# Second-phase weights of a three-stage network: raw slots, decoding order, store times and tile addresses

## Chip, cores and metric

The kernel runs on one core of a Trainium2 chip. The metric is the device time of one execution in microseconds (us); smaller is better.

## Reference

Three layers follow each other on 3072 tokens (4 batches of 768) with 384 features, all in float32:

```python
def _attn_ref(q, k, v, alpha):            # 8 heads of 48
    for t in range(S):
        state = alpha[:, :, t, :, None] * state + np.einsum('bhd,bhe->bhde', k[:, :, t], v[:, :, t])
        y[:, :, t] = np.einsum('bhd,bhde->bhe', q[:, :, t], state)
def _moe_ref(x, w_in, w_out):             # d_ff 2048
    h = x @ w_in
    return (h * (1.0 / (1.0 + np.exp(-h)))) @ w_out
def _moe2_ref(x, w_gate, w_val, w_out):   # d_ff 1536
    g = x @ w_gate
    return (g * (1.0 / (1.0 + np.exp(-g))) * (x @ w_val)) @ w_out
```

The result is `_moe2_ref(_moe_ref(_attn_ref(...)))`.

## The kernel before, in words

Every float32 product is made of three matmuls: both operands are split into a high part (rounded to the matmul's own float32 form) and the low rest, and high by high, low by high and high by low are added in PSUM. In names, `gh`, `ah` and `w` hold high parts and `gl` and `al` low ones.

**First phase.** Attention runs in chunks of 128 tokens. Beside it, and after it, runs the first feed-forward layer, in seven blocks of 4, 3, 3, 3, 3, 4 and 4 chunks, so its matmuls are 512 or 384 columns wide. One step of a block takes 128 of the 2048 hidden features: `g1` makes nine matmuls into `h` (L642, L643, L645), `act1` takes the silu on ACT twice (once rounded into `gh`, once in place) and leaves `gl` = `h` − `gh` to DVE (L264), and `g2` makes nine more (L676, L677 with `gh`, the last three at L679 with `gl`). After each half of a step, `slot` does whatever else is due. The first layer's weights `w` stay in SBUF.

**Second phase.** The gated layer is computed in three passes over 1024 tokens. A pass has 12 groups (`group`), each of 33 matmuls of 128x512 at L820, by a scheme of the Strassen kind: the stationary operands are sums and differences of weight blocks (tile `comb`, 128 x 2304, high and low half), the moving ones are sums and differences of tokens (`mov`). In a group, ACT copies (L854, L856, L867) and DVE adds (`u4` at L860, `v` at L873) stand between the matmuls, and `use` (L835, L838) makes the products `a` of the gate's silu and the values. Then the pass's output part follows: 24 steps of nine matmuls (`og`, L901), 216 in all, with the output weights `wo`; before each, `osplit` rounds one `a` tile to `ah` on ACT and takes `al` on DVE, or, in the first pass and for half of the steps, on POOL.

**The weights of the second phase.** They lie packed in DRAM, a float32 in 8 bytes, as 36 units of 128 x 768 words (24 of gate and value, 12 of output weights). A unit is loaded by SP (L610, 384 KB), then decoded by DVE in three integer steps over 128x384, all in SBUF (step 0 L47 `dec<-raw`, step 1 L52 `raw<-raw,dec`, step 2 L57 into `f` or back into `raw`). Two units make one `f` tile; POOL adds its blocks up (`combine`, L791 to L794), ACT rounds nine blocks into the high half of `comb` (`high_comb`, L798, 128x1152), POOL takes the low half (`low_comb`, L264, 128x1152), and SP stores `comb` to DRAM (L803, 1152 KB). The first pass uses `comb` as it is made; the other two load it back (`fetch_comb`, L807). An output unit is decoded, rounded by ACT (`high_wo`, L811) and subtracted by POOL (`low_wo`, 128x384).

**What orders this.** The order is written out by hand: each engine runs its instructions in the order in which the program issues them. `units2` (L1011) is one tick of the weights' work: each step of the chain advances by at most one unit in a tick, later steps first, and a step takes only what an earlier tick left. In a tick, a unit is loaded only if at most one loaded unit is still undecoded (`st["d2"] + 1`) and a slot of the three is free (`free + 2`). Ticks come from `slot` in the last two blocks of the first phase, from the first pass's groups through `spare` (one after `u4`, one at the group's end) and `need2`, and from its output part, in every second step (`b == 0`) or as often as the next `wo` needs. The load of the tokens of the next pass (`load_x1`, L708, tile `x1r` in the buffer `big1`) and the POOL and ACT work on them (`moving_steps`, L728) lie among them. `comb` tiles go in turn to two buffers of pool `sp2` and, every third, to `big0`.

## Time and profile before

| what | us |
|---|---|
| median of 3 executions | 1048.15 (1042.44 to 1048.27) |
| profiled execution, its own time | 1045.21 |
| its span | 1043.4 |
| PE busy in it | 977.0 |
| DVE, ACT, POOL busy | 516.9, 432.5, 273.3 |
| mean granted TensorE clock | 0.978 of full speed |

The profiled execution lies 2.9 us below the median of the three, and its span 1.8 us below its own time. PE is TensorE's matmuls, PEld its weight loads, and SPq is the DMA queue of SyncE. A matmul's own time in the trace overlaps the next one's start, so the pace of matmuls is read from start to start. A granted clock of 1.00 is 2.4 GHz, and a stretch at less is a mixture with 1.2 GHz.

### The profile page before, as it was taken

To read this page: it belongs to the slowest core of one execution; us is meant where nothing else is said; L and a number is where in the kernel's file an instruction comes from. 1 tells how busy PE (TensorE), PEld (TensorE's weight loads), DVE (VectorE), ACT (ScalarE), POOL (GpSimd) and SP (SyncE) were. 2 spreads that over 40 slices of the span, in tenths; PEclk is the share of its full clock that TensorE was granted. 3 is DMA by queue.
4 is the path that set the end of the run, shared out by engine and by line. 5 is a ranking of instruction groups with operands and counts; after the bars stand their busy time and mean duration, and the time that the engine had idled before them with its cause. 6 is when DMAs were issued, how large, how long until landed. Compare 5 with 4: busy or idle time off the path is not lost.

```text
span 1043.4 us, 14192 instructions
## 1 busy us (share of the span) xinstructions
PE 977.0 (94%) x5317; PEld 814.9 (78%) x5317; DVE 516.9 (50%) x912; ACT 432.5 (41%) x977; POOL 273.3 (26%) x347
## 2 busy tenths in 40 slices
PE   9889999999999999999599987988799999999995
PEld 5667798799999998888377765866588878788784
DVE  8889936444343553434342575664133354333432
ACT  3544435545454554433223543534233434433322
POOL 5434416343231441401330353254100020000000
PEclk9899999999999999999899998999899999999998
DMA  7664003222212222004620366441146420435001
GB/s 245 238 241 132 6 3 123 79 85 54 65 50 75 82 82 69 21 1 121 227 91 30 136 214 224 152 182 46 60 143 235 142 87 1 151 137 180 2 1 63
DMA packets 32780, 111.54 MB, mean 107 GB/s; under 512 B 3648, under 2 KB 7232, under 8 KB 28096
## 3 DMA queue, kind: packets, MB, share of 16 engines
q1 hardware_dynamic: 32224, 110.11, 31.2%
q8 instruction: 43, 0.70, 0.3%
q10 hardware_dynamic: 480, 0.46, 0.2%
q14 instruction: 33, 0.27, 0.1%
HBM read 85.00 MB, written 23.59 MB: 104 GB/s over the span
## 4 chain that ended last, share of the span: by engine, by line
PE 71%; DMA 10%; DVE 9%; issue 5%; POOL 3%; ACT 2%; SPq 0%; DVEq 0%; POOLq 0%; ACTq 0%
PE o L901 14%; PE u L820 13%; DMA raw<-in_w_dram 8%; PE p L820 7%; PE h L642 5%; PE x L679 5%; PE h L643 5%; PE h L645 5%; PE x L676 5%; PE x L677 5%; PE y L483 2%; PE y L505 2%; DVE f L57 2%; POOL w L264 2%; DVE dec L47 1%
## 5 line engine op out<-in xcount | busy, mean ns | idle before, releaser
L820 PE MATMUL u<-mov,comb 128*128 128x512 f32 x756 | 189.1, 397 | 12.7 <-DVE u L860 9.7
L820 PEld LDWEIGHTS u<-mov,comb 128*128 128x128 f32 x756 | 142.8, 191 | 48.2 <-DVE u L860 12.3
L901 PE MATMUL o<-ah,wo 128*128 128x512 f32 x432 | 140.2, 405 | 8.0 <-POOL wo L264 7.0
L642 PE MATMUL h<-x,w 128*128 128x384 f32 (+1 forms) x336 | 125.0, 372 | 1.7 <-DMA x<-y 1.6
L659 ACT ACTIVATE gh<-h 128x384 fp32r<-128x384 f32 (+1 forms) x112 | 59.7, 533 | 157.7 <-PE h L645 157.3
L676 PE MATMUL x<-gh,w 128*128 128x384 f32 (+1 forms) x336 | 122.9, 366 | 1.7 <-ACT gh L659 1.6
L643 PE MATMUL h<-x,w 128*128 128x384 f32 (+1 forms) x336 | 123.4, 367 | 0.0
L264 DVE TENSOR_TENSOR gl<-h,gh 128x384 fp32r<-128x384 f32 (+1 forms) x112 | 68.5, 612 | 108.5 <-ACT h L660 105.5
L677 PE MATMUL x<-gh,w 128*128 128x384 f32 (+1 forms) x336 | 122.0, 363 | 0.0
L820 PE MATMUL p<-mov,comb 128*128 128x512 f32 x432 | 110.8, 391 | 2.4 <-DVE a L838 2.3
L901 PEld LDWEIGHTS o<-ah,wo 128*128 128x128 f32 x432 | 83.2, 193 | 29.6 <-POOL wo L264 8.2
L679 PE MATMUL x<-gl,w 128*128 128x384 f32 (+1 forms) x336 | 88.2, 371 | 17.8 <-DVE gl L264 17.8
L820 PEld LDWEIGHTS p<-mov,comb 128*128 128x128 f32 x432 | 81.2, 188 | 21.0 <-DVE a L838 3.7
L901 PE MATMUL o<-al,wo 128*128 128x512 f32 x216 | 87.3, 404 | 4.3 <-DVE al L264 4.3
L891 ACT ACTIVATE ah<-a 128x512 fp32r<-128x512 f32 x72 | 45.5, 632 | 101.9 <-PE o L901 95.4
L645 PE MATMUL h<-x,w 128*128 128x384 f32 (+1 forms) x336 | 86.3, 365 | 0.0
L679 PEld LDWEIGHTS x<-gl,w 128*128 128x128 f32 x336 | 61.0, 189 | 29.3 <-DVE gl L264 23.1
L264 DVE TENSOR_TENSOR al<-a,ah 128x512 fp32r<-128x512 f32 x60 | 44.7, 745 | 72.0 <-ACT ah L891 69.6
L352 POOL TENSOR_TENSOR kq<-in,r 128x256 f32<-128x256 f32 x47 | 35.4, 754 | 157.6 <-DVE r L341 152.2
L47 DVE TENSOR_SCALAR dec<-raw 128x384 int32<-128x384 int32 x64 | 41.5, 648 | 63.7 <-DMA raw<-in_w_dram 62.5
L642 PEld LDWEIGHTS h<-x,w 128*128 128x128 f32 x336 | 64.0, 190 | 11.3 <-issue 5.4
L676 PEld LDWEIGHTS x<-gh,w 128*128 128x128 f32 x336 | 63.4, 189 | 10.1 <-ACT gh L659 4.2
(130 smaller groups left out, 1529.8 us busy)
## 6 DMA issues: line engine op xcount, KB each, us to landing
comb<-comb_d SPq DMA_DIRECT2D x24, 1152.0 KB, 5.2
raw<-in_w_dram SPq DMA_DIRECT2D x64, 384.0 KB, 3.9
in<-in_pk_dram SPq DMA_DIRECT2D x22, 770.5 KB, 4.2
comb_d<-comb SPq DMA_DIRECT2D x12, 1152.0 KB, 6.1
in_v<-in_pk_dram SPq DMA_DIRECT2D x24, 256.0 KB, 3.2
x1r<-x_d SPq DMA_DIRECT2D x6, 768.0 KB, 7.5
out_dram<-ob SPq DMA_DIRECT2D x18, 256.0 KB, 2.2
x_d<-x1e SPq DMA_DIRECT2D x4, 576.0 KB, 3.3
```

What stands on the lines that cost most here:

```text
L47: eng.tensor_scalar(out=tmp, in0=high, scalar1=3, scalar2=0x3FFFFFF8, op0=ALU.logical_shift_left, op1=ALU.bitwise_and,)
L264: eng.tensor_tensor(out=lo, in0=src, in1=hi.bitcast(F32), op=ALU.subtract)
L642: PE.matmul(acc, part(u, k), xh, start=(k == 0), stop=False)
L643: PE.matmul(acc, part(u, k, 1), xh, start=False, stop=False)
L645: PE.matmul(acc, part(u, k), xl, start=False, stop=(k == len(xk) - 1))
L659: ACT.activation(out=gh, in_=hb, func=AF.Silu)
L676: PE.matmul(x1_t[j][m], part(u, m), gh, start=(f == 0), stop=False)
L677: PE.matmul(x1_t[j][m], part(u, m, 1), gh, start=False, stop=False)
L679: PE.matmul(x1_t[j][m], part(u, m), gl, start=False, stop=(f == NF1 - 1))
L820: PE.matmul(acc, s[:, hs, i], x[:, hx], start=start and n == 0, stop=n == 2, skip_group_check=True,)
L891: ACT.activation(out=ah, in_=a, func=AF.Copy)
L901: PE.matmul(o_t[b][m], part(wo_t[f], m, l), x, start=(f == 0 and n == 0), stop=(f == NF2 - 1 and n == 2),)
```

## The change

The packed weights get one tile `raw2` with four slots, in the buffer `big1`, which `x1r` leaves for `big0`; all `comb` tiles now come from pool `sp2`. In a tick up to two loads are issued, as far as slots are free (`free + 3` with the next one). A unit is decoded if it was loaded at least two ticks earlier, and then all three integer steps are issued in a row (`decode2`). The store of `comb` becomes a step of its own (`keep_comb`), one tick after `low_comb`. In the first pass, a group of even number makes both its ticks after `u4`, and one of odd number makes one there and none at its end; ticks that are lacking come from `need2` ahead of the next group. In the first pass's output part every step has a tick. The small tiles `lim`, `cnt`, `ones` and `tot` share a tile of tag `y3`.

```diff
@@ -237,6 +237,8 @@
     x1_d = dram.tile([128, KT, NT], F32, name="x1_d")
     comb_d = dram.tile([NF2, 128, 18 * 128], F32, name="comb_d")
     cp = ctx.enter_context(tc.tile_pool(name="cp", bufs=1))
+    edge = ctx.enter_context(tc.tile_pool(name="edge", bufs=1, side="right"))
+    edge.tile([128, 120], F32, name="edge_r")
     wstack = ExitStack()
     wp = wstack.enter_context(tc.tile_pool(name="wp", bufs=2 * NF1, side="right"))
     ps = ctx.enter_context(tc.tile_pool(name="ps", bufs=1, space=PSUM))
@@ -259,6 +261,7 @@
     sums = cp.tile([128, 2, NCH], F32, name="sums")
     ysum = cp.tile([128, 2, NCH], F32, name="ysum")
     warm = cp.tile([128, 1], F32, name="warm")
+    cp.tile([128, 112], F32, name="edge")
 
     def sub(eng, lo, src, hi):
         eng.tensor_tensor(out=lo, in0=src, in1=hi.bitcast(F32), op=ALU.subtract)
...
@@ -300,7 +302,7 @@
         if n >= NCH:
             return
         if n not in in_t:
-            t = ap.tile([128, A_W + 2 * W], F32, tag="in", name=f"in{n}")
+            t = ap.tile([128, A_W + 2 * W + 123], F32, tag="in", name=f"in{n}")[:, :A_W + 2 * W]
             in_t[n] = t[:, :A_W], t[:, A_W:].rearrange("p (x r t) -> p x r t", x=2, r=NP)
             raw_in[n] = t
         t = raw_in[n]
...
@@ -702,7 +708,7 @@
     x1r_t, mov = {}, {}
 
     def load_x1(p):
-        r = x1r_t[p] = big(1, f"x1r{p}").rearrange("p (b k t) -> p b k t", b=2, k=KT)
+        r = x1r_t[p] = big(0, f"x1r{p}").rearrange("p (b k t) -> p b k t", b=2, k=KT)
         for b in range(2):
             t = 1024 * p + 512 * b
             SP.dma_start(out=r[:, b], in_=x1_d[:, :, t:t + 512])
@@ -751,13 +757,10 @@
             lambda: low(T4),
         ]
 
-    f_t, comb_t, wo_t = {}, {}, {}
+    f_t, comb_t, wo_t, loaded, ticks = {}, {}, {}, {}, [0]
 
     def comb_place(u):
-        if u % 3 == 2:
-            t = big(0, f"comb{u}", F32R)[:, :18 * 128]
-        else:
-            t = pools2["s"].tile([128, 18 * 128], F32R, tag=f"comb{u % 3}", name=f"comb{u}", bufs=1)
+        t = pools2["s"].tile([128, 18 * 128], F32R, tag=f"comb{u % 3}", name=f"comb{u}", bufs=1)
         comb_t[u] = t.rearrange("p (x i e) -> p x i e", x=2, i=9)
         return t
 
@@ -769,13 +772,15 @@
         return w2[2 * q + i, :, m * DM:(m + 1) * DM]
 
     def load2(w):
-        raw = pools2["s"].tile([128, 2 * DM], I32, tag="raw", name=f"raw2_{w}", bufs=3)
-        load_unit(("2", w), w2_src(w), raw)
-
-    def decode2(w, step):
+        load_unit(("2", w), w2_src(w), pools2["raw"][:, w % 4])
+        loaded[w] = ticks[0]
+
+    def decode2(w):
         key = "2", w
-        if step < 2 or w >= 2 * NF2:
-            return decode_unit(key, step)
+        decode_unit(key, 0)
+        decode_unit(key, 1)
+        if w >= 2 * NF2:
+            return decode_unit(key, 2)
         u, i = divmod(w, 2)
         if i == 0:
             f_t[u] = pools2["s"].tile([128, 10, 128], F32, tag="f", name=f"f{u}", bufs=2)
@@ -800,7 +805,9 @@
     def low_comb(u):
         t = comb_t[u]
         sub(POOL, t[:, 1], f_t[u][:, 1:], t[:, 0])
-        SP.dma_start(out=comb_d[u], in_=t.bitcast(F32).rearrange("p x i e -> p (x i e)"))
+
+    def keep_comb(u):
+        SP.dma_start(out=comb_d[u], in_=comb_t[u].bitcast(F32).rearrange("p x i e -> p (x i e)"))
 
     def fetch_comb(u):
         t = comb_place(u)
@@ -858,7 +865,9 @@
         term(x2, u, S2, T2)
         x3 = bank(i3, f"u4_{n}")
         DVE.tensor_tensor(out=x3, in0=x2, in1=s5, op=ALU.add)
-        spare(0)
+        spare()
+        if u % 2 == 0:
+            spare()
         term(x1, u, A12, B21)
         term(x1, u, A13, B31)
         use(p, u, 0, 0, x1)
@@ -872,7 +881,6 @@
         v = pools2["r"].tile([128, 512], F32, tag="v", name=f"v_{n}", bufs=2)
         DVE.tensor_tensor(out=v, in0=x2, in1=s5, op=ALU.add)
         use(p, u, 1, 1, v)
-        spare(1)
 
         def rest():
             term(x4, u, A22, T4)
...
@@ -1011,25 +1019,26 @@
     def units2(room=3):
 
         was = dict(st)
+        ticks[0] += 1
 
         def step(key, limit, fn):
-            if was[key] < limit and st[key] == was[key]:
+            if was[key] < limit:
                 fn(st[key])
                 st[key] += 1
 
+        step("sp", was["s2"], keep_comb)
         step("s2", was["h2"], low_comb)
         step("sw", was["hw"], low_wo)
         step("h2", min(was["c2"], room), high_comb)
         if "r" in pools2:
             step("hw", was["f2"] - NW, high_wo)
         step("c2", min(was["f2"] // 2, NF2), combine)
-        step("e2", was["d2"], lambda w: decode2(w, 1))
-        if st["e2"] == st["d2"]:
-            step("d2", was["l2"], lambda w: decode2(w, 0))
-        if was["f2"] >= NW or was["f2"] // 2 < st["s2"] + 2:
-            step("f2", was["e2"], lambda w: decode2(w, 2))
+        w = st["f2"]
+        if w < st["l2"] and loaded[w] < ticks[0] - 1 and (w >= NW or w // 2 < st["s2"] + 2):
+            decode2(w)
+            st["f2"] += 1
         free = st["f2"] if st["f2"] < NW else NW + st["sw"]
-        up_to("l2", min(st["d2"] + 1, free + 2), load2, NU2)
+        up_to("l2", min(st["l2"] + 1, free + 3), load2, NU2)
 
     def need2(u, room):
         while st["s2"] <= u:
@@ -1109,10 +1118,9 @@
         astack.close()
         pools2["s"] = ctx.enter_context(tc.tile_pool(name="sp2", bufs=2))
 
-        sp = pools2["s"]
-        lim = sp.tile([128, 2], F32, name="lim", bufs=1)
-        cnt = sp.tile([128, 2 * NCH], F32, name="cnt", bufs=1)
-        ones = sp.tile([128, 128], F32, name="ones", bufs=1)
+        pools2["raw"] = big(1, "raw2", I32).rearrange("p (u c) -> p u c", u=4)
+        small = mp.tile([128, 2 * 512], F32, tag="y3", name="small", bufs=1)
+        ones, cnt, lim = small[:, :128], small[:, 128:128 + 2 * NCH], small[:, 192:194]
         POOL.memset(ones, 1.0)
         flat = [t.rearrange("p a n -> p (a n)") for t in (sums, ysum)]
         DVE.tensor_tensor(out=flat[1], in0=flat[1], in1=flat[1], op=ALU.mult)
...
@@ -1203,7 +1211,7 @@
         for u in range(NF2):
             if p == 0:
                 need2(u, u + 1)
-            group(p, u, (lambda k: units2(u + 3)) if p == 0 else (lambda k: None))
+            group(p, u, (lambda: units2(u + 3)) if p == 0 else (lambda: None))
             if p and u + 2 < NF2 and u:
                 fetch_comb(u + 2)
             if u == 6 and p + 1 < NPAIR:
@@ -1219,7 +1227,7 @@
         for n, (f, b) in enumerate(order):
             if n + 1 < len(order):
                 osplit(p, *order[n + 1])
-            if p == 0 and b == 0:
+            if p == 0:
                 units2()
                 while st["sw"] <= f:
                     units2()
```

The hunks left out pad the `r` and `g` tiles of the attention from 258 to 384 columns, put the tiles of pool `ac` in another order (`qh` and `ql` first, `ones` and `rc` last), and rename keys and small tiles. Lines of the new program are 2 to 9 higher from L240 on.

By the paddings the tiles move. Start addresses in a partition, in bytes, from the build of the two programs:

| tile | before | after |
|---|---|---|
| `w` (32 tiles of 3072 bytes from) | 131,040 | 130,560 |
| `wo` (from) | 192,480 | 192,000 |
| tokens `x`, in `big0` / `big2` | 4,672 / 16,960 | 5,120 / 17,408 |
| `gh` | 47,168 | 47,616 |
| `comb` | 4,672, 75,584, 84,800 | 66,048, 75,264, 84,480 |
| `mov` (from) | 102,208 | 101,888 |

Those of `w` and `wo` lay 32 bytes past a multiple of 64 before; the others of the table lay at multiples of 64. Now all are multiples of 512.

Three places in the order of instructions. First DVE in the last block of the first phase, between the second and the third `gl` (`gl6_1`, `gl6_2`; a `raw2_N` before is the tile of unit N, `dec2_N` unit N's scratch, `f` the decoded pair). Before:

```order
L264 TENSOR_TENSOR gl6_1_5118<-h6_1_5107,gh6_1_5117 128x512
L52 SCALAR_TENSOR_TENSOR raw2_3_5085<-raw2_3_5085,dec2_3_5102 128x384
L47 TENSOR_SCALAR dec2_4_5127<-raw2_4_5105 128x384
L57 SCALAR_TENSOR_TENSOR f1_5129<-raw2_2_5051 128x384
L52 SCALAR_TENSOR_TENSOR raw2_4_5105<-raw2_4_5105,dec2_4_5127 128x384
L47 TENSOR_SCALAR dec2_5_5151<-raw2_5_5131 128x384
L57 SCALAR_TENSOR_TENSOR f1_5129<-raw2_3_5085 128x384
L264 TENSOR_TENSOR gl6_2_5167<-h6_2_5156,gh6_2_5166 128x512
```

After:

```order
L267 TENSOR_TENSOR gl6_1_5122<-h6_1_5111,gh6_1_5121 128x512
L47 TENSOR_SCALAR dec2_3_5128<-raw2_5016 128x384
L52 SCALAR_TENSOR_TENSOR raw2_5016<-raw2_5016,dec2_3_5128 128x384
L57 SCALAR_TENSOR_TENSOR f1_5108<-raw2_5016 128x384
L47 TENSOR_SCALAR dec2_4_5153<-raw2_5016 128x384
L52 SCALAR_TENSOR_TENSOR raw2_5016<-raw2_5016,dec2_4_5153 128x384
L57 SCALAR_TENSOR_TENSOR f2_5156<-raw2_5016 128x384
L267 TENSOR_TENSOR gl6_2_5170<-h6_2_5159,gh6_2_5169 128x512
```

Six integer steps stand there in either kernel. Before, they belong to four units, 2 to 5, and the last of them to be loaded, 5, has its step 0 ahead of `gl6_2`; now they are units 3 and 4 whole, and nothing ahead of `gl6_2` needs unit 5.

Second SP's queue from the first loads of the second phase on (`x1_d` is the first layer's output, `x1r0` the tokens of the first pass read back, `comb0` the first combined weights). Before:

```order
L610 DMA raw2_3_5085<-in_w2_dram 128x768
L688 DMA x1_d_63<-x1e5_5096 384x1x512
L610 DMA raw2_4_5105<-in_w2_dram 128x768
L610 DMA raw2_5_5131<-in_w2_dram 128x768
L708 DMA x1r0_5145<-x1_d_63 128x3x512 x2
L610 DMA raw2_6_5154<-in_w2_dram 128x768
L803 DMA comb_d_64<-comb0_5148 128x2304
L610 DMA raw2_7_5182<-in_w2_dram 128x768
```

After, from the first load of a unit on:

```order
L616 DMA raw2_5016<-in_w2_dram 128x768 x6
L694 DMA x1_d_63<-x1e5_5096 384x1x512
L616 DMA raw2_5016<-in_w2_dram 128x768 x2
L714 DMA x1r0_5145<-x1_d_63 128x3x512 x2
L616 DMA raw2_5016<-in_w2_dram 128x768
L810 DMA comb_d_64<-comb0_5126 128x2304
L616 DMA raw2_5016<-in_w2_dram 128x768 x2
L810 DMA comb_d_64<-comb1_5175 128x2304
```

Before, four units were loaded ahead of the store to `x1_d` and the seventh behind the loads of `x1r0`; now six are, and eight ahead of `x1r0`, and the store of `comb0` comes behind the ninth.

Third DVE in group 6 of the first pass, from `u4` to `v`. Before, with step 1 of unit 20, step 0 of unit 21 and step 2 of unit 19 between them:

```order
L860 TENSOR_TENSOR u4_0_6_6039<-u2_0_6_6026,s5_0_6_6024 128x512
L52 SCALAR_TENSOR_TENSOR raw2_20_5973<-raw2_20_5973,dec2_20_6010 128x384
L47 TENSOR_SCALAR dec2_21_6044<-raw2_21_6014 128x384
L57 SCALAR_TENSOR_TENSOR f9_6012<-raw2_19_5940 128x384
L873 TENSOR_TENSOR v_0_6_6073<-u2_0_6_6026,s5_0_6_6024 128x512
```

After, with two units (17 and 18) whole between them:

```order
L867 TENSOR_TENSOR u4_0_6_5996<-u2_0_6_5983,s5_0_6_5981 128x512
L47 TENSOR_SCALAR dec2_17_6001<-raw2_5016 128x384
L52 SCALAR_TENSOR_TENSOR raw2_5016<-raw2_5016,dec2_17_6001 128x384
L57 SCALAR_TENSOR_TENSOR f8_5970<-raw2_5016 128x384
L47 TENSOR_SCALAR dec2_18_6011<-raw2_5016 128x384
L52 SCALAR_TENSOR_TENSOR raw2_5016<-raw2_5016,dec2_18_6011 128x384
L57 SCALAR_TENSOR_TENSOR f9_6014<-raw2_5016 128x384
L882 TENSOR_TENSOR v_0_6_6041<-u2_0_6_5983,s5_0_6_5981 128x512
```

Six integer steps stand ahead of `v` where three stood; the last unit that `v` is behind is 18 where it was 21.

## Rows read from the trace of the kernel before

**Rows 1.** The page, part 1: busy time, share of span, instructions
```profile
PE 977.0 (94%) x5317; PEld 814.9 (78%) x5317; DVE 516.9 (50%) x912; ACT 432.5 (41%) x977; POOL 273.3 (26%) x347
```

**Rows 2.** Stretches: PE, PEld, DVE, ACT, POOL busy, PEclk, DMA share, GB/s
```profile
480.00:540.00 60.00, 46.12 (x178) 35.76 (x177) 29.23 (x51) 16.30 (x27) 22.70 (x27) 0.89 0.49 165
540.00:560.00 20.00, 20.00 (x88) 16.08 (x87) 6.44 (x10) 8.13 (x15) 1.04 (x1) 1.00 0.00 1
580.00:620.00 40.00, 36.28 (x154) 28.01 (x152) 26.65 (x39) 18.17 (x27) 19.81 (x18) 1.00 0.56 188
720.00:740.00 20.00, 14.55 (x47) 10.43 (x45) 5.91 (x11) 5.87 (x11) 4.87 (x4) 0.83 0.00 1
```

**Rows 3.** Waits of PE, 450 to 570: us, times, longest
```profile
PE x L679 <- DVE gl L264: 13.9, 4, 6.9
```

**Rows 4.** Timeline of DVE: start, us, instruction, idle time before it
```profile
506.71 0.36 DVE L47 TENSOR_SCALAR dec<-raw 128x384 int32<-128x384 int32 x1 [5.13 <-DMA raw<-in_w_dram]
507.45 0.69 DVE L264 TENSOR_TENSOR gl<-h,gh 128x512 fp32r<-128x512 f32 x1
```

**Rows 5.** Waits of the DMA queue, whole span
```profile
SPq L610 <- DVE f L57: 106.9, 24, 8.7
```

**Rows 6.** Timeline of PE: first matmuls of five stages
```profile
569.33 0.40 PE L820 MATMUL p<-mov,comb 128*128 128x512 f32 x1
...
679.70 0.39 PE L901 MATMUL o<-ah,wo 128*128 128x512 f32 x1
...
748.18 0.40 PE L820 MATMUL p<-mov,comb 128*128 128x512 f32 x1
...
839.12 0.39 PE L901 MATMUL o<-ah,wo 128*128 128x512 f32 x1
...
890.06 0.63 PE L820 MATMUL p<-mov,comb 128*128 128x512 f32 x2
```

**Rows 7.** Chain that ended last, 586 to 646, by line
```profile
by line: DMA raw<-in_w_dram 77.3%; DVE f L57 14.3%; DVE dec L47 6.3%; issue 3.0%; DVEq L47 0.3%
```

**Rows 8.** Waits of PE, 680 to 749
```profile
PE o L901 <- POOL wo L264: 7.0, 3, 2.6
```

**Rows 9.** Timeline of PE: nine matmuls 128x512, nine 128x384
```profile
250.60 0.34 PE L642 MATMUL h<-x,w 128*128 128x384 f32 x1
...
252.18 0.32 PE L427 MATMUL s<-qh,kh 128*128 128x352 f32 x1
...
542.03 0.39 PE L642 MATMUL h<-x,w 128*128 128x512 f32 x1
...
544.13 0.39 PE L676 MATMUL x<-gh,w 128*128 128x512 f32 x1
```

**Rows 10.** Chain, 752 to 764: start, us, matmuls with combined weights
```profile
760.29 2.72 PE u L820 x12
```

**Rows 11.** Timeline of POOL and DVE at 596 us
```profile
596.12 2.66 POOL L264 TENSOR_TENSOR comb<-f,comb 128x1152 fp32r<-128x1152 f32 x1 [2.31 <-ACT comb L798]
...
596.67 2.53 DVE L52 SCALAR_TENSOR_TENSOR raw<-raw,dec 128x384 int32<-128x384 int32 x1
```

**Rows 12.** Decode step 1: shortest, median, longest ns
```profile
L52 DVE SCALAR_TENSOR_TENSOR raw<-raw,dec x64: 527/547/2533, 35.6 to 721.8; 128x384 int32<-128x384 int32 x64
```

**Rows 13.** Groups of POOL, 680 to 749: busy us, mean ns
```profile
L264 POOL TENSOR_TENSOR al<-a,ah 128x512 fp32r<-128x512 f32 x12 | 16.1, 1342 | 41.7 <-ACT ah L891 27.4 <-DVE a L838 14.3
...
L728 POOL TENSOR_TENSOR x1r<-x1r 128x512 f32<-128x512 f32 x4 | 5.9, 1465 | 1.9 <-DVE mov L264 1.8
```

**Rows 14.** Timeline of DVE in a group of pass 1
```profile
751.47 0.70 DVE L860 TENSOR_TENSOR u<-u,s 128x512 f32<-128x512 f32 x1 [2.80 <-PE u L820]
755.52 0.69 DVE L873 TENSOR_TENSOR v<-u,s 128x512 f32<-128x512 f32 x1 [3.35 <-PE u L820]
```

**Rows 15.** Timeline of PE at a low granted clock
```profile
727.89 1.05 PE L901 MATMUL o<-ah,wo 128*128 128x512 f32 x2
728.75 0.63 PE L901 MATMUL o<-al,wo 128*128 128x512 f32 x1
```

## Prediction before the run

> **What bounds the kernel now.** I read the page first. PE is busy for 977.0 of 1043.4 us [rows 1], so most of the time is matmuls and only what PE loses, or the pace of a matmul, can pay. Then I read PE by stretches and by marks, to see where it falls behind its own pace elsewhere.
>
> A, the last block of the first phase: 88 matmuls start in 20 us at 540 to 560, a stretch with no gap, but only 178 in the 60 us before it, where three times 88 would be 264 [rows 2]. The 86 that lack, at 20/88 us each, are 19.5 us. The wait is PE for `gl` (13.9 us, four times, the longest 6.9) [rows 3], and DVE's timeline shows why: `gl` at 507.45 stands behind a `dec` that had kept DVE idle for 5.13 us until its raw unit landed [rows 4]. DVE runs in order, so a late DMA holds up a product that has nothing to do with it. The rest of the 19.5 is the granted clock, 0.89 there [rows 2].
>
> B, the 12 groups of pass 0: from 569.33 to 679.70, 110.4 us, where the same groups of pass 1 take 839.12 − 748.18 = 90.9 [rows 6]. 19.4 us are lost. The chain through 586 to 646 is raw loads for 77.3% [rows 7]: load, decode, next load. The queue waits for the last step of a decode 24 times, 106.9 us in all [rows 5]; a load is issued only when the slot before it is decoded, and the decode follows a tick later, so the latency of each load stands in the chain.
>
> C, the output part of pass 0: 748.18 − 679.70 = 68.5 against 890.06 − 839.12 = 50.9 in pass 1 [rows 6]; 17.5 us lost. PE waits 7.0 us for `wo` from POOL [rows 8], and the granted clock is 0.83 at 720 to 740 [rows 2].
>
> A, B and C are 56.4 us together. A weight unit is behind each.
>
> **The slots and the decode.** The change takes loads out of that chain: four slots, up to two loads a tick, and a decode that is issued only two ticks after its load. A group makes two ticks, so a load has about one group, 7.6 us (90.9/12); in A and C a tick is nine matmuls, 2.1 us [rows 9], and a load has 4.2. A load in the chain of B took 3.6 us: 77.3% of 60 us are 46.4, for two units in each 9.2 us (110.4/12), 13 in all. So the load fits in each stage, barely in A and C, and I expect the wait for DMA in A and B to go nearly whole. Late next are three things.
>
> In A, as DVE's order around `gl6_2` shows, `gl` still stands behind six integer steps, now of units loaded two ticks before. A step 0 and a step 2 take 0.74 us from start to start (506.71 to 507.45) [rows 4], and step 1 is alike to step 2, so a unit takes about 1.2 and two 2.4; PE has nine matmuls of 2.1 us as cover. Residual 2, bounds 0 and 6 (two of the four waits staying, at three each). On SP, the store to `x1_d` and the tokens `x1r0` come behind two loads more than before, 384 KB each, at the 188 GB/s of 580 to 620 [rows 2] 4.1 us; the tokens are first read several half steps later, so this is hidden, and if it weren't, the first group would be late by those 4.1 us, which the bounds hold. A gives 19.5 − 2 = 17.5.
>
> In B, an even group now has both its ticks between `u4` and `v`. Their starts are 4.05 us apart in pass 1 [rows 14], and 0.7 of that is `u4` itself, so 3.3 us lie free for two decodes of 1.2 each. That fits, as in group 6's order above, until POOL is at a `comb` subtract. Then one decode step takes as long as that subtract: step 1 at 596.67 took 2.53 beside POOL's 2.66 at 596.12 [rows 11], against a median of 547 ns [rows 12]. Two decodes and one such hold are 2.4 + 2.0 = 4.4, so `v` comes 1.1 late, and later where the subtract begins late. ACT's `u` copy is behind `v`, and the next group behind that. I take 1.5 us a group for four of the even groups and 0.5 for four odd ones: 8, bounds 0 and 16 (six even groups by 2.66). The two DMA streams leave room: a group loads 2 x 384 KB and stores 1152 KB, 1.9 MB in 7.6 us, which is 258 GB/s if each group did both; 188 GB/s were moved at 580 to 620 [rows 2], so a store may lag, and it has a tick more to start. B gives 19.4 − 8 = 11.4.
>
> In C, a tick in each of the 24 steps lets `wo` units flow at up to one a tick where one in two is needed. But on POOL's queue stand also half of the `al` (1342 ns) and four subtracts of the next pass's tokens (1465 ns) [rows 13], and `al` is wanted by the very next step. A step has 2.1 us of matmuls; an `al` of 1.34 behind a `wo` of about 1 us and a token subtract is late by 1 to 2 us in some of the 12 steps. Also `comb` 0 to 2 for pass 1 stand in the same SP queue as the raw loads. I take 6 us, bounds 1 and 12, and 0.9 for the copies of the output tile that stand ahead of pass 1's first group once PE comes to it without a stall. C gives 17.5 − 6.9 = 10.6.
>
> `x1r` in `big0`, `comb` out of it, and the store a tick later I cost at nothing: a pass has 91 us of groups to hide its tokens, and what is stored is read again only in pass 1. The later store also no longer stands in SP's queue waiting for POOL with loads behind it. If that cover were gone, a store would hold back one load, 3.6 us. The small tiles cost nothing.
>
> Sum of the three: 17.5 + 11.4 + 10.6 = 39.5 us, by the bounds 21.5 to 54.5.
>
> **The addresses.** This part acts where PE never waits. Nine 128x512 matmuls with `w` take 544.13 − 542.03 = 2.10 us, 233.3 ns each [rows 9]. Twelve with `comb` take 2.72, 226.7 each [rows 10]; the shape is the same. In the build `w` and `wo` start 32 bytes past a multiple of 64, `comb` and the moving tiles at multiples of 64. If that is the difference, it goes. 864 matmuls with `w` and 648 with `wo` are 512 wide; 288 of the 864 lie in the first block, where PE waits for weights and attention and gains little. 1224 x 6.7 ns are 8.2 us. The 1152 that are 384 wide take 1.58/9 = 175.6 ns [rows 9]; no row shows them with an aligned weight. Between no gain and the same share (6.7 of 233, 5.0 ns, 5.8 us) I take half, 2.9. Together 11. The bounds: the pace of `comb` could go the other way, 1188 x 6.7 ns = 8 us lost; at best 1512 x 6.7 ns + 5.8 = 16 us gained.
>
> A row that lets me doubt it: weight loads are hidden behind the matmuls, and nothing here shows an address at work alone. The Trainium skill says in "SBUF — State Buffer", section "Door 1: The DMA port swizzle (why `[64,N]` ≈ `[32,N]`)", that accesses within one line of 16 bytes run at full bandwidth and those that cross to another line pay. By that rule 131,040 is as good as 130,560, both being multiples of 16, and the sum would be without the 11 us. The trace has two paces for one shape, which that rule does not explain, so I go by the trace, and keep the rule as a rival.
>
> **The forecast.** 1045.2 (the profiled execution's own time) − 39.5 − 11 = 994.7. The median of the runs lies 2.9 above that execution, so 997.6, given as 998.
>
> **Rivals.**
> First, the addresses give nothing, because the pace comes from the kind of accumulation and not from where the tiles lie: the weights' part alone gives 998 + 11 = 1009. For it: no row isolates the cause. Against: two paces, and an address difference that goes with them.
>
> Second, DVE and POOL hold each other up. All integer steps now come in blocks, close to POOL's subtract of the pair before. If each even group pays a whole subtract (16 us in B), A keeps 4 and C its bound of 12.9, then 15.5 + 3.4 + 4.6 = 23.5 are left: 1048.15 − 23.5 − 11 = 1013.6, or 1025 without the addresses. For it: [rows 11]. Against: the median of step 1 over all 64 units is 547 ns [rows 12], so most miss the subtract. The same page of the Trainium skill says under "Who interferes with whom" that a DVE instruction with two SBUF inputs and a GpSimd instruction that reads SBUF exclude each other for a whole instruction; the trace's 2.53 us agrees.
>
> Third, the pace drops once more, by another 6.7 ns on all 1512 + 1188 matmuls of 512 columns (multiples of 512 where `comb` had multiples of 64): 18 us, so 980. For it: nothing but that `comb` too moves to a rounder address.
>
> Fourth, slower: the waits do not vanish but become short and regular in B and C, behind `v` and `al`, and the clock is not granted. At 727.89 two matmuls take 0.86 us, 0.43 each against 0.233 at full clock [rows 15], so each of the 612 matmuls of B and C costs 0.20 more. The gain of 50 us is gone from 250 matmuls on; with half of the 612 it is 61, and the time 1059. For it: 720 to 740 has 0.83 already. Against: at 580 to 620 PE did 154 matmuls with gaps, where 176 would fit, and kept 1.00 [rows 2].
>
> **Chances.** The forecast 0.42, the addresses without effect 0.26, DVE against POOL 0.19, the second drop 0.07, the clock 0.06. About 1% is what a measurement of this kernel can tell from no change. All but the fourth and a third of the second lie more than 1% (10.5 us) below 1048, that third (0.06) near it: faster 0.88, within 1% 0.06, slower 0.06. The range is 981 to 1028. Its top is the sum at its lower bound with no gain from the addresses (1048.15 − 21.5 = 1026.7); its bottom is the sum near its upper bound with most of the addresses' 16 (1048.15 − 54.5 − 12.6). The clock, most of the second drop and a part of DVE against POOL lie outside.
>
> **What would show it.** Right: no `dec` waits for a raw unit of the second phase; 480 to 540 has close to 250 matmuls; pass 0's groups take about 99 us and its output part about 58; nine matmuls with `w` take 2.04 us. Wrong step by step: the 2.10 us stay (first rival); DVE's `raw<-raw,dec` has many of 2.5 us and PE waits for `v` or `u` in pass 0 (second); twelve matmuls with `comb` fall below 2.6 us (third); PEclk falls in 580 to 750 (fourth). If PE still waits for `gl` behind a load, the ticks are too short for the DMA and A's step is wrong.

## The result, and the profile after

| | before | after |
|---|---|---|
| median, us | 1048.21 (1042.44 to 1048.37, 4 runs) | 1012.99 (1011.36 to 1013.77, 4 runs) |
| ratio | | 0.9677 (95%: 0.9647 to 0.9707) |
| span of the profiled execution | 1043.4 | 1009.6 |
| mean granted clock | 0.978 | 0.987 |

The change saves 35.2 us where 50 were forecast. Of the kernels below, `split_ticks` had one execution of five at 3295.98 us, which is set aside as slow (the other four took 997.0 to 999.1).

The page after, its busy times and the chain that ended last, by line:

```profile
PE 960.6 (95%) x5317; PEld 808.6 (80%) x5317; DVE 532.3 (53%) x912; ACT 431.1 (43%) x977; POOL 278.7 (28%) x347
...
PE u L827 14%; PE o L909 13%; PE p L827 8%; PE h L648 5%; PE h L649 5%; PE h L651 5%; PE x L682 5%; PE x L683 5%; PE x L685 5%; DVE dec L47 3%; DVE raw L52 2%; PE y L489 2%; PE y L511 2%; POOL w L267 2%; DVE a L845 1%
```

PE is busy for 16 us less than in [rows 1], though it runs the same 5317 matmuls, and raw loads are gone from the chain; DVE's decode (`dec`, `raw`) stands in it instead. The first matmuls of the stages that [rows 6] showed, on PE's timeline after (start, us, instruction):

```profile
546.42 0.39 PE L827 MATMUL p<-mov,comb 128*128 128x512 f32 x1
...
652.00 0.61 PE L909 MATMUL o<-ah,wo 128*128 128x512 f32 x2
...
715.36 0.62 PE L827 MATMUL p<-mov,comb 128*128 128x512 f32 x2
...
807.30 0.61 PE L909 MATMUL o<-ah,wo 128*128 128x512 f32 x2
...
856.88 0.62 PE L827 MATMUL p<-mov,comb 128*128 128x512 f32 x2
```

From these marks and [rows 6], in us:

| stage | before | after | change |
|---|---|---|---|
| up to the first group | 569.33 | 546.42 | −22.9 |
| B, groups of pass 0 | 110.4 | 105.6 | −4.8 |
| C, output part of pass 0 | 68.5 | 63.4 | −5.1 |
| groups of pass 1 | 90.9 | 91.9 | +1.0 |
| output part of pass 1 | 50.9 | 49.6 | −1.3 |

The stretches of A, B and C after (PE, PEld, DVE, ACT, POOL busy, PEclk, DMA share, GB/s):

```profile
477.30:546.40 69.10, 68.56 (x303) 56.47 (x302) 38.30 (x59) 26.76 (x47) 25.62 (x27) 1.00 0.40 143
546.00:652.00 106.00, 95.63 (x400) 74.84 (x399) 73.10 (x102) 46.90 (x75) 41.01 (x39) 0.98 0.52 182
652.00:716.00 64.00, 56.41 (x220) 43.59 (x219) 40.11 (x48) 24.47 (x43) 34.60 (x26) 0.92 0.30 105
```

The last block of the first phase starts 0.5 us into the first of these stretches, 69.1 us with PE busy for 68.6. It has next to no gap left and full clock: A is gone, and no wait of PE for `gl` stands there. In B and C PE is still idle for 10 and 8 us. Its waits there (us, times, longest; first 545 to 652, then 652 to 716):

```profile
PE u L827 <- ACT u L863: 5.3, 5, 1.7
PE u L827 <- ACT u L876: 2.6, 1, 2.6
...
PE o L909 <- DVE al L267: 6.8, 5, 2.9
```

The queue still waits for decodes before it can issue a load, 106.9 us before [rows 5] and now 58.0 and 37.2:

```profile
SPq L616 <- DVE f L57: 58.0, 20, 7.1
...
SPq L616 <- DVE dec L47: 37.2, 4, 21.8
```

But these waits hold nobody up. DVE's waits over the whole span before have the row below; after, no decode waits for a load any more.

```profile
DVE dec L47 <- DMA raw<-in_w_dram: 62.5, 30, 5.1
```

What is late in B is mostly ACT's `u` copy at L863, which stands behind `v` (the one wait for L876 is taken up in the part on the prediction). DVE's timeline shows an even group, then an odd one (u4 is at L867, `v` at L882):

```profile
581.73 0.70 DVE L867 TENSOR_TENSOR u<-u,s 128x512 f32<-128x512 f32 x1
582.34 1.91 DVE L47 TENSOR_SCALAR dec<-raw 128x384 int32<-128x384 int32 x1
584.28 0.56 DVE L52 SCALAR_TENSOR_TENSOR raw<-raw,dec 128x384 int32<-128x384 int32 x1
584.88 0.56 DVE L57 SCALAR_TENSOR_TENSOR f<-raw 128x384 int32<-128x384 int32 x1
585.35 0.35 DVE L47 TENSOR_SCALAR dec<-raw 128x384 int32<-128x384 int32 x1
...
587.10 0.68 DVE L882 TENSOR_TENSOR v<-u,s 128x512 f32<-128x512 f32 x1
...
590.53 0.70 DVE L867 TENSOR_TENSOR u<-u,s 128x512 f32<-128x512 f32 x1 [2.76 <-PE u L827]
591.14 2.81 DVE L47 TENSOR_SCALAR dec<-raw 128x384 int32<-128x384 int32 x1
593.98 0.56 DVE L52 SCALAR_TENSOR_TENSOR raw<-raw,dec 128x384 int32<-128x384 int32 x1
594.58 0.56 DVE L57 SCALAR_TENSOR_TENSOR f<-raw 128x384 int32<-128x384 int32 x1
595.05 0.68 DVE L845 TENSOR_TENSOR a<-p,sg 128x512 f32<-128x512 f32 x1
595.65 0.68 DVE L845 TENSOR_TENSOR a<-u,sg 128x512 f32<-128x512 f32 x1
596.25 0.68 DVE L882 TENSOR_TENSOR v<-u,s 128x512 f32<-128x512 f32 x1
```

And POOL's timeline, the two subtracts of `comb` in the same stretch:

```profile
581.35 2.68 POOL L267 TENSOR_TENSOR comb<-f,comb 128x1152 fp32r<-128x1152 f32 x1 [8.50 <-ACT comb L803]
...
591.05 2.68 POOL L267 TENSOR_TENSOR comb<-f,comb 128x1152 fp32r<-128x1152 f32 x1 [3.14 <-ACT comb L803]
```

Step 0 takes 1.91 and 2.81 us and ends just behind POOL's subtract; the third step 0 of these rows, issued while POOL is idle, takes 0.35. So `v` starts 5.4 us after `u4` in the one and 5.7 in the other, where a group without weights' work has 4.05 [rows 14]. The Trainium skill says in "SBUF — State Buffer", section "Who interferes with whom", that a `tensor_scalar`, too, can enter a mode that takes the port pair shared with GpSimd, and that the one who issues second waits for the whole instruction; step 0 is a `tensor_scalar` with one input tensor, and these rows agree.

In C, DVE's groups between 652 and 690 (busy us, mean ns, idle time before):

```profile
L52 DVE SCALAR_TENSOR_TENSOR raw<-raw,dec 128x384 int32<-128x384 int32 x8 | 8.3, 1042 | 0.8
L57 DVE SCALAR_TENSOR_TENSOR raw<-raw 128x384 int32<-128x384 int32 x8 | 7.6, 944 | 0.3
L267 DVE TENSOR_TENSOR al<-a,ah 128x512 fp32r<-128x512 f32 x7 | 7.1, 1016 | 4.3 <-ACT ah L899 4.3
L47 DVE TENSOR_SCALAR dec<-raw 128x384 int32<-128x384 int32 x8 | 5.5, 692 | 0.0
```

Steps 0, 1 and 2 take 692 + 1042 + 944 ns, 2.7 us a unit, where 0.35 + 0.56 + 0.56 stood in B beside an idle POOL: POOL's `wo`, `al` and token subtracts run beside them, and the long steps end just behind one of those; a step of nine matmuls is 2.05. With one unit in each step, `al` falls behind.

### The profile page after: what moved, and what is told of

It reads as the page before. It is cut to its first block, busy times and chain, and to the rows that moved or that the text cites. A ratio compares the mean times of both kernels' runs of the same rounds, so it can differ in the third digit from the quotient of the medians.

```text
span 1009.6 us, 14182 instructions
## 1 busy us (share of the span) xinstructions
PE 960.6 (95%) x5317; PEld 808.6 (80%) x5317; DVE 532.3 (53%) x912; ACT 431.1 (43%) x977; POOL 278.7 (28%) x347
## 4 chain that ended last, share of the span: by engine, by line
PE 73%; DVE 13%; issue 5%; ACT 3%; POOL 3%; DMA 2%; SPq 0%; DVEq 0%; POOLq 0%; ACTq 0%
PE u L827 14%; PE o L909 13%; PE p L827 8%; PE h L648 5%; PE h L649 5%; PE h L651 5%; PE x L682 5%; PE x L683 5%; PE x L685 5%; DVE dec L47 3%; DVE raw L52 2%; PE y L489 2%; PE y L511 2%; POOL w L267 2%; DVE a L845 1%
## 5 line engine op out<-in xcount | busy, mean ns | idle before, releaser
L827 PE MATMUL u<-mov,comb 128*128 128x512 f32 x756 | 186.3, 392 | 12.5 <-ACT u L863 9.1
L909 PE MATMUL o<-ah,wo 128*128 128x512 f32 x432 | 136.4, 397 | 0.5 <-ACT ah L899 0.5
L267 DVE TENSOR_TENSOR gl<-h,gh 128x384 fp32r<-128x384 f32 (+1 forms) x112 | 68.6, 612 | 113.9 <-ACT h L666 110.7
L648 PE MATMUL h<-x,w 128*128 128x384 f32 (+1 forms) x336 | 122.9, 366 | 1.7 <-DMA x<-y 1.6
L649 PE MATMUL h<-x,w 128*128 128x384 f32 (+1 forms) x336 | 121.1, 360 | 0.0
L827 PEld LDWEIGHTS p<-mov,comb 128*128 128x128 f32 x432 | 81.5, 189 | 20.2 <-DVE a L845 2.9
L685 PE MATMUL x<-gl,w 128*128 128x384 f32 (+1 forms) x336 | 85.5, 362 | 4.1 <-DVE gl L267 4.1
L651 PE MATMUL h<-x,w 128*128 128x384 f32 (+1 forms) x336 | 84.6, 360 | 0.0
L267 DVE TENSOR_TENSOR al<-a,ah 128x512 fp32r<-128x512 f32 x60 | 45.4, 757 | 70.6 <-ACT ah L899 68.2
L458 DVE TENSOR_TENSOR pt<-s,mask 128x256 f32<-128x256 f32 x92 | 38.1, 418 | 60.3 <-PE s L435 59.1
```

What stands on the lines that cost most here:

```text
L267: eng.tensor_tensor(out=lo, in0=src, in1=hi.bitcast(F32), op=ALU.subtract)
L458: DVE.tensor_tensor(out=pt, in0=s_t[g][0], in1=mask.rearrange("p (o t) -> p o t", o=1).to_broadcast([128, 2, C]), op=ALU.mult,)
L648: PE.matmul(acc, part(u, k), xh, start=(k == 0), stop=False)
L649: PE.matmul(acc, part(u, k, 1), xh, start=False, stop=False)
L651: PE.matmul(acc, part(u, k), xl, start=False, stop=(k == len(xk) - 1))
L685: PE.matmul(x1_t[j][m], part(u, m), gl, start=False, stop=(f == NF1 - 1))
```

## The experiments

The ratio is to the kernel before in the same job, whose median was 1042 to 1044 us in these jobs (1048.2 in that of the first two rows), so kernels of different jobs are compared by their ratios. The stages are from the profile of each kernel, first matmul to first matmul, in us; "last block" runs from its first to the first group's matmul.

| kernel | median, us | ratio (95%) | last block | B | C |
|---|---|---|---|---|---|
| before | 1048.2 | 1 | 88.9 | 110.4 | 68.5 |
| after | 1013.0 | 0.9677 (0.9647 to 0.9707) | 68.7 | 105.6 | 63.4 |
| before_w64 | 1044.7 | 1.0004 (0.9975 to 1.0033) | 89.6 | 111.1 | 70.8 |
| no_edges | 1019.1 | 0.976 (0.9715 to 0.9804) | 70.0 | 105.4 | 64.5 |
| all_64 | 1010.1 | 0.969 (0.9645 to 0.9735) | 68.6 | 105.5 | 63.4 |
| low_dve | 1016.3 | 0.9737 (0.9694 to 0.978) | 68.6 | 111.4 | 63.4 |
| split_ticks | 998.3 | 0.9565 (0.9522 to 0.9608) | | | |
| split_ticks_2 | 999.6 | one run | 68.6 | 98.6 | 59.1 |
| out_b0 | 1004.7 | 0.9623 (0.9588 to 0.9658) | 68.6 | 105.6 | 55.2 |
| split_b0 | 997.7 | 0.9561 (0.9535 to 0.9587) | 68.6 | 98.5 | 57.4 |
| three_slots | 1011.3 | 0.968 (0.9643 to 0.9718) | 68.5 | 105.5 | 62.5 |
| one_tick | 1014.2 | 0.9719 (0.9693 to 0.9745) | 69.8 | 105.4 | 63.8 |
| spread | 1003.7 | 0.9614 (0.9588 to 0.964) | 70.6 | 100.6 | 59.3 |
| store_w0 | 1012.5 | one run | 69.1 | 105.6 | 63.6 |

**The addresses.** The first kernel is the one before with only `w` and `wo` moved:

```diff
+    edge = ctx.enter_context(tc.tile_pool(name="edge", bufs=1, side="right"))
+    edge.tile([128, 8], F32, name="edge_r")
```

> The kernel before, with w and wo moved down by 32 bytes (131,008 and 192,448, multiples of 64) and nothing else. Theory of the addresses: the 128x512 matmuls with w and wo go from 231-233 to 227 ns, the 128x384 from 177 to 173, and the time falls by 7 to 9 us (ratio 0.991 to 0.994). Rival (the pace is not the address of the weights, but came with other parts of the change): no change, pace stays at 231-233 ns.

No change: the pace stayed. The second is the changed kernel without the two edge tiles (`edge_r` and the one in `cp`), which moves `w` and `wo`, and all other tiles too, to 64 bytes past a multiple of 512:

> The changed kernel with the two edge tiles taken out: w and wo back at 32 bytes past a multiple of 64, all others at 64 past a multiple of 512. Theory of the addresses: w and wo matmuls back at 231-233 ns, about 1020 us (7 to 9 more than the changed kernel), matmuls with comb stay at 227 ns. Rival: 1013.

1019.1 us; the stages with `w` and `wo` are longer, the groups are not. The third kernel differs from the second by `w` and `wo` alone: with `edge_r` of 104 columns and no tile in `cp` they lie as all its other tiles do:

> The changed kernel with every tile, w and wo too, at 64 past a multiple of 512. If the pace hangs on where the weights lie against the moving tiles (the same offset): 128x512 with w and wo at 227 ns as in the changed kernel, 1013 us. If it hangs on the weights' own distance from a multiple of 512 (or 128): 231-233 ns, 1019 us.

1010.1 us, as fast as the changed kernel with nothing at a multiple of 512. Six matmuls of the last block, start to start, on PE's timeline of no_edges:

```profile
530.80 0.40 PE L679 MATMUL x<-gh,w 128*128 128x512 f32 x1
...
532.20 0.40 PE L682 MATMUL x<-gl,w 128*128 128x512 f32 x1
```

1.40 us, 233 ns each. And of all_64:

```profile
529.90 0.39 PE L682 MATMUL x<-gh,w 128*128 128x512 f32 x1
...
531.26 0.39 PE L647 MATMUL h<-x,w 128*128 128x512 f32 x1
```

1.36 us, 227 ns each. The mean distance of successive matmuls in the output parts (gaps over 260 ns left out), with the start of weights and of moving tiles past a multiple of 512:

| kernel | `wo` / moving, bytes | ns |
|---|---|---|
| before | 480 / 64 | 233.3 |
| before_w64 | 448 / 64 | 233.1 |
| no_edges | 480 / 64 | 233.4 |
| store_w0 | 0 / 64 | 229.0 |
| all_64 | 64 / 64 | 227.2 |
| after | 0 / 0 | 227.3 |

So the address does set the pace, but neither a multiple of 64 for the weights nor one of 512 for all is the condition. In these rows it is fastest where weights and moving tiles lie alike, and all but so where they differ by 64; `comb`, which lies at 64 or 320 against `mov` at 320 in the kernel before, has 227.5 there, and in passes 1 and 2 the third of the groups that has it at 64, so 256 bytes off, is as fast as the others (226.7). What the rule is stays open.

**What stands ahead of `v`.** The low half of `comb` on DVE in pass 0:

```diff
-        sub(POOL, t[:, 1], f_t[u][:, 1:], t[:, 0])
+        sub(DVE if "r" in pools2 else POOL, t[:, 1], f_t[u][:, 1:], t[:, 0])
```

> The changed kernel with the low half of comb taken on DVE instead of POOL in pass 0. Theory (in pass 0's groups DVE's decode waits for POOL's subtract, and v and the next group wait for the decode): step 0 after u4 falls from a mean of 1193 ns to under 500, the 12 groups from 105.6 to 94-99 us, the time by 6 to 11 us. Rival (it is the amount of DVE work ahead of v, not the hold): DVE gets some 1.5 us more a group, and the groups take 105 to 120 us, no faster than the changed kernel.

111.4 us in the groups: the rival's time, by a path that neither had. DVE's groups, 545 to 660:

```profile
L267 DVE TENSOR_TENSOR comb<-f,comb 128x1152 fp32r<-128x1152 f32 x9 | 12.2, 1351 | 0.0
...
L47 DVE TENSOR_SCALAR dec<-raw 128x384 int32<-128x384 int32 x19 | 8.3, 438 | 0.0
```

Step 0 is down to a mean of 438 ns, as the theory has it, and `v` comes late by 7.3 us over the 12 groups instead of 12.9 (sum of its distance from `u4`'s start, less 4.05 each). But the subtract takes 1.35 us of DVE, and where `need2` runs it at a group's end, PE waits for `comb` itself:

```profile
PE p L827 <- DVE comb L267: 7.7, 3, 2.6
```

Only the ticks, with everything else left:

```diff
         spare()
-        if u % 2 == 0:
-            spare()
...
         use(p, u, 1, 1, v)
+        spare()
```

> The changed kernel with pass 0's ticks where they were before: one after u4, one at the group's end, in every group. Theory of the hold: the one step 0 after u4 still waits for POOL's subtract (2.7 us) but the second decode no longer stands ahead of v; groups 98 to 103 us, time 1006 to 1011. Rival (DVE is simply full in these groups): groups stay at 105 us, time 1013.

998.3 us; by the ratios, 0.9565 against 0.9677, 12 us less than the changed kernel, where 2 to 7 were expected. Its trace, from one more run:

> The same kernel as split_ticks (one tick after u4, one at the group's end), for its trace. Theory (what stands ahead of v on DVE, decode and hold together, sets the groups of pass 0): one unit ahead of v, groups near 92 to 95 us where the changed kernel has 105.6; the rest of the gain in the output part. Rival (the gain lies elsewhere, in the output part or the last block of the first phase): groups stay above 102.

B is 98.6, short of the 92 to 95 expected, and C 59.1. DVE's timeline, a group of pass 0 (u4 at L867, `v` at L880):

```profile
582.37 0.69 DVE L867 TENSOR_TENSOR u<-u,s 128x512 f32<-128x512 f32 x1
582.97 2.04 DVE L47 TENSOR_SCALAR dec<-raw 128x384 int32<-128x384 int32 x1
585.04 0.56 DVE L52 SCALAR_TENSOR_TENSOR raw<-raw,dec 128x384 int32<-128x384 int32 x1
585.64 0.56 DVE L57 SCALAR_TENSOR_TENSOR f<-raw 128x384 int32<-128x384 int32 x1
586.21 0.69 DVE L880 TENSOR_TENSOR v<-u,s 128x512 f32<-128x512 f32 x1
586.82 0.35 DVE L47 TENSOR_SCALAR dec<-raw 128x384 int32<-128x384 int32 x1
```

Step 0 is held for 2.04 us as before, but the second unit comes behind `v`, at 586.82. `v` starts 3.84 us behind `u4` here, in time; in the odd groups it is 5.76, as a unit, a hold and two products `a` stay ahead of it there. Over all groups it is 7.0 us late. So hold and work fill the gap together, and one unit fewer is enough to gain.

**The output part.**

```diff
-            if p == 0:
+            if p == 0 and b == 0:
                 units2()
```

> The changed kernel with a tick only in every second step of pass 0's output part, as before. Theory (in this part DVE decodes units faster than wo is needed, each step held by POOL's subtracts, and al on DVE comes late): the part falls from 63.4 to 55-60 us and the time by 3 to 8. Rival (POOL's sum of al, wo and token subtracts is what limits it): 63 us, no change.

C is 55.2, 8.2 less, and the ratio 0.9623, 6 us less. PE's wait for `al`, 6.8 us in the changed kernel, over 640 to 705:

```profile
PE o L909 <- DVE al L267: 3.0, 3, 2.2
```

So it is the rate of the decodes, not POOL's sum, which is the same (34.5 us busy, 34.6 in the changed kernel). A part of the 8.2 goes with the clock: 0.97 was granted here over C, 0.92 there. Both edits in one kernel:

> The changed kernel with both tick edits: one tick after u4 and one at the group's end in pass 0, and a tick only in every second step of its output part. If the two losses are separate (decode ahead of v in the groups, decode ahead of al in the output part): groups 98 to 99 us as in split_ticks_2, output part near 55 as in out_b0, 990 to 995 us. If they are one loss that each edit removes by itself: 998.

997.7 us: B as in split_ticks_2, C 57.4 and not 55. The two are not separate: with ticks at the groups' ends 20 units instead of 18 are decoded before the output part begins. Why C is longer here than in out_b0 isn't shown. The sum of B and C is 155.9 against 157.7 (split_ticks_2), 160.8 (out_b0) and 169.0 (after). This kernel and split_ticks are faster than both the kernel before and the changed one.

**Slots, waiting rule, decoding in one go, store.** Three slots:

```diff
-        load_unit(("2", w), w2_src(w), pools2["raw"][:, w % 4])
+        load_unit(("2", w), w2_src(w), pools2["raw"][:, w % 3])
...
-        up_to("l2", min(st["l2"] + 1, free + 3), load2, NU2)
+        up_to("l2", min(st["l2"] + 1, free + 2), load2, NU2)
```

> The changed kernel with three raw slots instead of four. Theory (what the fourth slot gives is a load that is never waited for): loads come a tick later, decodes in the last block and in pass 0 fall behind, 2 to 10 us slower than the changed kernel. Rival (the two ticks between load and decode do it, three slots are enough): 1013 us, the same.

The same time as with four. Decodes wait for loads again, but for little; DVE's waits, whole span:

```profile
DVE dec L47 <- DMA raw<-in_w_dram: 3.2, 5, 1.0
```

The two-tick rule (`loaded[w] < ticks[0] - 1` becomes `< ticks[0]`):

> The changed kernel, but a unit may be decoded one tick after its load instead of two. Theory (the waiting rule is what keeps DVE from standing idle for a load, and with it gl in the last block): the last block goes from 68.7 us towards the 88.9 of the kernel before, 5 to 20 us slower in all, with DVE waiting for raw units again. Rival (the loads are ahead by then in any case, since two go out in a tick): 1010 to 1014, no waits.

1014.2 us, an interval that overlaps the changed kernel's, with one wait:

```profile
DVE dec L47 <- DMA raw<-in_w_dram: 1.3, 1, 1.3
```

The decoding steps in three successive ticks, as before, all else as changed (the steps have counters `d2`, `e2`, `f2` again):

> The changed kernel with the three decoding steps of a unit in three successive ticks, as before, and the slots, loads and two-tick rule of the changed one. Theory (decoding in one go matters little by itself; what counts is how many integer steps stand ahead of v and al): within 4 us of the changed kernel, DVE not waiting for loads. Rival (a slot held two ticks longer starves the loads): the last block and the groups grow, 5 us or more slower.

1003.7 us, further off than the 4 expected, and to the better, though decodes wait for loads again (4.3 us, five times) and the last block is 1.9 us longer: decoding in one go costs 7 us by the ratios (0.9677 against 0.9614). B is 100.6 and C 59.3. `v` is late by 10.0 us over the groups instead of 12.9. A part of it is plain: a step that reads what the step before wrote starts later. In the changed kernel a unit takes 0.38 + 0.67 + 0.48 us from start to start:

```profile
574.85 0.35 DVE L47 TENSOR_SCALAR dec<-raw 128x384 int32<-128x384 int32 x1
575.23 0.56 DVE L52 SCALAR_TENSOR_TENSOR raw<-raw,dec 128x384 int32<-128x384 int32 x1
575.90 0.56 DVE L57 SCALAR_TENSOR_TENSOR f<-raw 128x384 int32<-128x384 int32 x1
576.38 0.69 DVE L845 TENSOR_TENSOR a<-p,sg 128x512 f32<-128x512 f32 x1
```

In spread, step 2 follows another unit's step 0 after 0.27, and takes 0.47 to the next start:

```profile
598.20 0.36 DVE L47 TENSOR_SCALAR dec<-raw 128x384 int32<-128x384 int32 x1
598.47 0.55 DVE L57 SCALAR_TENSOR_TENSOR f<-raw 128x384 int32<-128x384 int32 x1
598.94 0.68 DVE L843 TENSOR_TENSOR a<-u,sg 128x512 f32<-128x512 f32 x1
```

Last, the store in the tick of `low_comb` again, and, read apart from it, the address of the moving tiles (no tile in `cp`):

```diff
-        step("sp", was["s2"], keep_comb)
         step("s2", was["h2"], low_comb)
+        step("sp", st["s2"], keep_comb)
```

> The changed kernel with two edits whose effects are read apart: the store of comb in the tick of low_comb again, and all tiles but w and wo back at 64 past a multiple of 512 (w and wo stay at multiples of 512). Pace: if it hangs on the weights lying like the moving tiles, 128x512 with wo at 233 ns; if on the weights' own address, 227. Store: if its later tick keeps loads from standing behind it in the queue, the last block and pass 0's groups are 2 to 8 us longer than the changed kernel's 68.7 and 105.6; if the loads have time enough, they are the same within 1.

Last block and groups are the same within 0.5 us, so the later store buys nothing by itself; the pace came out between the two cases (229.0, table above).

## Why the prediction was right in its direction, and 15 us too fast

**A was right.** 17.5 us and A's share of the addresses were forecast; the last block is 20.2 us shorter, and PE waits for `gl` nowhere in it. But the reason had too many parts. The four slots and the two ticks between load and decode were taken to be the cure; with three slots, or one tick, or the store back, or the decode in three ticks, A stays cured (68.5 to 70.6 us). What all of these kernels keep is the loading rule, a load whenever a slot is free instead of one unit ahead of the decode. By elimination that is the cure; it was not undone alone, and as each other part was undone by itself, two of them might also stand in for each other.

**B was mis-sized.** The step that failed is "I take 1.5 us a group for four of the even groups and 0.5 for four odd ones: 8". After, `v` is 1.0 to 2.0 us late behind two decodes in four even groups, 5.3 together, near the 6 of the working. But in three odd groups it is 1.6 to 1.7 late, 4.9 together where 2 were taken, as the two products `a` stand ahead of it there behind a hold and a decode. And in group 10 it is 2.7 late by a path that the working didn't have: the second tick after `u4` puts the rounding of an output unit (`high_wo`, L818) on ACT ahead of the `u` copy at L876, and it waits for the decode, which DVE does under a hold. ACT's timeline:

```profile
639.13 0.55 ACT L818 ACTIVATE wo<-raw 128x384 fp32r<-128x384 f32 x1 [4.08 <-DVE raw L57]
```

That is 12.9 in all; B lacks 14.7 to the 90.9 of pass 1 before. Eight of the ten groups with a decode behind `u4` pay a hold (step 0 of 1.6 to 2.8 us), as POOL's subtract starts 0.1 to 1.5 us ahead of it in each of them; and a unit decoded in one go takes 1.5 us, not 1.2. The median of step 1 [rows 12] could not show this: in pass 0's groups before it is 0.55 us as well, though four of the 16 steps took 1.8 to 2.5. And `v` was 8.6 us late over these groups already before, under the waits for loads.

**C was mis-sized** as well: "I take 6 us, bounds 1 and 12". It lacks 13.8 to the 49.6 of the later output parts, beyond the bound, and pass 1's groups take 1.0 longer. The 6 was put on `al` behind other work on POOL's queue. It was `al` on DVE's, behind units decoded earlier than `wo` needs them; out_b0 shows 8.2 us of it, with the clock's part. PE waited for `al` on DVE before, too, over 680 to 749, where the prediction read only the wait for `wo`:

```profile
PE o L901 <- DVE al L264: 3.8, 2, 2.5
```

The sum of C also put the clock at nothing. 0.92 was granted over its 63.4 us (0.93 over C before), which is some 5 us, an estimate by the share that wasn't granted (0.08 of 63.4).

**The addresses** were forecast at 11 and gave 9.3 by the traces of no_edges and after (stages with `w` and `wo`: 5.4 us up to the first group, 1.2, 1.4 and 1.3 in the output parts), 8.7 by their ratios (0.0083 of 1045 us). The cause named, a start 32 bytes past a multiple of 64, was wrong, as before_w64 shows. By the rule on lines of 16 bytes, which the prediction has from the Trainium skill ("SBUF — State Buffer", section "Door 1: The DMA port swizzle (why `[64,N]` ≈ `[32,N]`)"), they would have given nothing.

The sum: against the 50.5 of the four parts (17.5 + 11.4 + 10.6 + 11), A is +1.4 (20.2 less 1.3 for its share of the addresses, against 17.5), B −6.6, C −6.7 (5.1 less 1.2 for its addresses, against 10.6), the addresses −1.7 and pass 1's groups −1.0; that leaves 35.9. The spans of the two profiled executions differ by 33.8: ahead of the last block 1.5 us less than the addresses' share was gained, and pass 2's groups are 0.6 longer. The medians differ by 35.2.

**The rivals.** The first (addresses give nothing) and the third (a second drop) are out by the pace. The second, DVE against POOL, given 0.19, is what happened in B and C: 16 and 12.9 lost were its terms, 14.7 and 13.8 were measured, and its 1014 is met, though A kept nothing of the 4 it had. Its sign, many `raw<-raw,dec` of 2.5 us, did not come: in B the longest takes 1.27, as the hold falls on step 0. Its mechanism alone isn't enough, as low_dve shows: without the hold the groups got longer. The fourth stayed small in B (granted clock 0.98 over the groups, some 2 us by the same estimate; 1.00 in split_ticks_2) and took some 5 us in C, about as much as in the kernel before.

## What to carry to other kernels

When a wait for a DMA is removed, look at what the work that waited then stands ahead of: here whole decodes moved in front of `v` and `al`, and gave back part of the gain; spreading the same work over the group was worth 12 us more. Price a hold between two engines by whether both come to it at the same point of every round, since then it comes nearly every time, and a median, in which a few long steps leave no trace, does not tell its size. And test each part of a compound change alone: the slots, the waiting rule and the later store gave nothing, decoding in one go cost, and what was gained came from the addresses and, by elimination and not by a test of its own, the loading rule.

## What was not expected of the hardware

The start-to-start time of fp32r matmuls of 512 columns depends on how weights and moving operand lie in SBUF: 227.2 to 233.4 ns for starts that differ by 0 to 416 bytes within 512, at the same shape and full clock; it does not simply grow with the difference, as 256 bytes cost nothing (`comb`) and 416 cost 6 ns. A DVE integer step on 128x384 that reads the result of the step just ahead starts 0.38 us behind it where an independent one starts 0.27 behind.
